# Fixed buffers for the transposed K chunks, and a writer that waits for the readers alone

## The chip, the core and the metric

The kernel runs on one core of a Trainium2 chip. The metric is the device time of one execution in microseconds (us).

## The reference

One decoding step: attention over a long cache, and an MLP beside it, mixed by a gate.

```python
B, Sq, D = 2, 1, 1024;  H, Sk, Dh = 32, 16384, 128      # all bf16
q = (x @ wq) per head
scores = einsum("bhqd,bhkd->bhqk", q, k_cache) * Dh**-0.5
a = (softmax(scores) @ v_cache) @ wo
b = mixer MLP of x with w1, w2, w3, w4
out = g * a + (1 - g) * b
```

The K and V caches hold 537 MB (2 x 2 x 32 x 16384 x 128 elements of 2 bytes). Every byte is used once, so the kernel has little arithmetic for each byte.

## The kernel before

The work is cut into 32 tiles, each of one batch and two heads. A tile loads 8.39 MB of K and 8.39 MB of V into a ring of three big buffers. K comes with its positions on the partitions, so VectorE transposes it in 32 x 32 blocks, in 16 chunks (`m`) of 128 x 1024 words, and TensorE multiplies each transposed chunk T with q in four matmuls. T has two buffers from a pool, so transpose `m` has to wait until the matmuls have read chunk `m - 2`.

```python
    tpool = ctx.enter_context(tc.tile_pool(name="tpool", bufs=2))

    def t_tile(shape, dtype, name="T"):
        return tpool.tile(shape, dtype, tag="T", name=name)
    # ... cut ...
        for m in range(NM):                               # NM = 16, per tile
            T = t_tile([P, 2, CJ, 32], FP32)
            nc.vector.transpose(
                out=T[:].rearrange("p w j s -> p j w s"),
                in_=Kw[:, m * CW : (m + 1) * CW].rearrange("p (j w e) -> p j w e", w=2, e=32),
            )
            # ... Tb is T seen as bf16 ...
            for v in range(4):
                nc.tensor.matmul(S[:], lhsT=z[:, v, NM - 1 - m : NM - 1 - m + P],
                                 rhs=Tb[:, v // 2, :, v % 2], ...)
```

After the 16 chunks come the softmax on 128 x 512 scores and, when V is there, 64 matmuls with V. Each load is issued when its buffer is free: the next V after the last transpose of a K, the next K after the matmuls of a V.

## Time and profile before

| | before |
|---|---|
| time, median | 1337.5 us |
| span in the profile | 1335.6 us |
| bytes moved | 573.3 MB, 429 GB/s |
| VectorE busy | 57%, of which the transposes of K 612 us |
| TensorE busy | 60% |

First the page of the kernel before. The rows of 40 digits cut the span into equal slices; a 9 stands for 90% or more. Below them are the DMA queues with their packets, megabytes, and share of the time of 16 DMA engines.

```profile
DMA  9999999999999999999999999999999999999997
GB/s 409 438 436 432 423 440 426 437 440 426 434 434 435 439 426 429 436 434 438 438 425 432 429 438 436 438 430 432 428 440 432 433 430 433 438 438 429 430 423 303
DMA packets 12725, 573.29 MB, mean 429 GB/s; under 512 B 1784, under 2 KB 1792, under 8 KB 2560
## 3 DMA queue, kind: packets, MB, share of 16 engines
q1 hardware_dynamic: 12664, 572.54, 99.2%
q8 instruction: 39, 0.64, 0.2%
q14 instruction: 14, 0.11, 0.0%
```

The DMA engines are full from the first slice to the last but one. Queue q1 carries the kernel's loads and alone fills 99.2% of the 16 engines.

The Trainium skill, "DMA: Bandwidth & Descriptors", section "Where 436 GB/s comes from", gives 435.2 GB/s as what the 16 ports between a core's DMA engines and its on-chip memory can carry. The trace agrees: most slices lie between 423 and 440 GB/s, and from one K to the next it is 435 GB/s (16.78 MB in 38.6 us).

Next the timeline of one tile: start, duration, engine and line, work, and in brackets how long the engine had idled and for what.

```profile
615.63 0.33 SPq L107 DMA_DIRECT2D Vn<-in_A_v_cache_dram  x1
...
620.38 0.33 SPq L96 DMA_DIRECT2D Kn<-in_A_k_cache_dram  x1
...
634.09 2.37 DVE L325 STREAM_TRANSPOSE T<-Kn 128x1024 f32<-128x1024 f32 x2 [7.35 <-DMA Kn<-in_A_k_cache_dram]
...
638.85 15.64 DVE L325 STREAM_TRANSPOSE T<-Kn 128x1024 f32<-128x1024 f32 x13 [0.22 <-PE S L333]
...
672.68 2.37 DVE L325 STREAM_TRANSPOSE T<-Kn 128x1024 f32<-128x1024 f32 x2 [7.06 <-DMA Kn<-in_A_k_cache_dram]
```

V is issued at 615.63 us, K at 620.38 us. VectorE idles 7.35 us until K lands at 634.09, and the next K lands 38.6 us later. The load issued at 615.63 stands behind one that is in flight until 634.09, so it could have been issued 18 us later without the engines running dry. The 13 transposes in 15.64 us (1.203 us each) run back to back.

Last, the line of the transposes: its instructions, those of the queue's sequencer (DVEq), and what VectorE idled for in front of it.

```profile
L325 DVE STREAM_TRANSPOSE T<-Kn x512: 1201/1245/1247, 43.5 to 1276.4; 128x1024 f32<-128x1024 f32 x171
L325 DVEq EVENT_SEMAPHORE  x449: 21/21/21, 44.8 to 1275.2; - x150
...
  DMA Kn<-in_A_k_cache_dram: 208.5, 30
```

### The profile page before, as it was taken

To read this page: it belongs to the slowest core of one execution; us is meant where nothing else is said; L and a number is where in the kernel's file an instruction comes from. 1 tells how busy PE (TensorE), PEld (TensorE's weight loads), DVE (VectorE), ACT (ScalarE), POOL (GpSimd) and SP (SyncE) were. 2 spreads that over 40 slices of the span, in tenths; PEclk is the share of its full clock that TensorE was granted. 3 is DMA by queue.
4 is the path that set the end of the run, shared out by engine and by line. 5 is a ranking of instruction groups with operands and counts; after the bars stand their busy time and mean duration, and the time that the engine had idled before them with its cause. 6 is when DMAs were issued, how large, how long until landed. Compare 5 with 4: busy or idle time off the path is not lost.

```text
span 1335.6 us, 11856 instructions
## 1 busy us (share of the span) xinstructions
PE 796.7 (60%) x4954; PEld 353.6 (26%) x5017; DVE 759.0 (57%) x998; ACT 27.2 (2%) x68; POOL 13.3 (1%) x40
## 2 busy tenths in 40 slices
PE   2576655676656665555666555576655556665564
PEld 0223222332225222222222222232222222222232
DVE  1677665466652665555666555566655556665540
ACT  0000000000000000000000000000000000000000
POOL 0000000000000000000000000000000000000000
PEclk9788877788776877778887777888777788877775
DMA  9999999999999999999999999999999999999997
GB/s 409 438 436 432 423 440 426 437 440 426 434 434 435 439 426 429 436 434 438 438 425 432 429 438 436 438 430 432 428 440 432 433 430 433 438 438 429 430 423 303
DMA packets 12725, 573.29 MB, mean 429 GB/s; under 512 B 1784, under 2 KB 1792, under 8 KB 2560
## 3 DMA queue, kind: packets, MB, share of 16 engines
q1 hardware_dynamic: 12664, 572.54, 99.2%
q8 instruction: 39, 0.64, 0.2%
q14 instruction: 14, 0.11, 0.0%
q10 hardware_dynamic: 8, 0.00, 0.0%
HBM read 572.53 MB, written 0.00 MB: 429 GB/s over the span
## 4 chain that ended last, share of the span: by engine, by line
DVE 25%; PE 25%; DMA 23%; issue 13%; another core or an unknown queue 12%; ACT 1%; SPq 0%; ACTq 0%; POOL 0%
DVE T L325 19%; PE S L333 14%; DMA Kn<-in_A_k_cache_dram 13%; PE O L377 7%; DMA wt<-in_B_w_dram 4%; DMA Vn<-in_A_v_cache_dram 3%; DMA wo<-in_A_wo_dram 3%; PE misc L212 2%; DVE Os L392 2%; PE misc L514 1%; ACT Pr L361 1%; DVE PT L365 1%; DVE mx L354 1%; PE misc L400 1%
## 5 line engine op out<-in xcount | busy, mean ns | idle before, releaser
L333 PE MATMUL S<-T,z 128*128 128x512 bf16 x1985 | 582.6, 422 | 333.4 <-DVE T L325 313.7
L325 DVE STREAM_TRANSPOSE T<-Kn 128x1024 f32<-128x1024 f32 x512 | 612.3, 1229 | 260.9 <-DMA Kn<-in_A_k_cache_dram 208.5
L333 PEld LDWEIGHTS <-z 128*128 128x128 bf16 x2048 | 211.0, 104 | 691.7 <-issue 530.0
L377 PE MATMUL O<-Vn,PT 128*32 128x512 bf16 x2048 | 121.4, 390 | 3.1 <-DMA Vn<-in_A_v_cache_dram 3.1
L377 PEld LDWEIGHTS <-PT 128*32 128x32 bf16 x2048 | 75.2, 142 | 48.2 <-issue 20.3
L388 DVE TENSOR_SCALAR Os<-O,xmask 128x128 f32<-128x128 f32 x32 | 11.2, 351 | 101.2 <-PE O L377 101.2
L212 PE MATMUL misc<-rs,ones_f 128*128 128x2 f32 x64 | 17.9, 349 | 79.1 <-DVE rs L408 79.1
L361 ACT ACTIVATE Pr<-S,nb 128x512 bf16<-128x512 f32 x32 | 22.0, 687 | 1199.1 <-DVE nb L356 1161.4
L344 DVE TENSOR_REDUCE m<-S 128x1 f32<-128x512 f32 x32 | 22.1, 692 | 36.9 <-PE S L333 36.9
L400 PE MATMUL misc<-asel,Os 128*128 128x2 f32 x64 | 12.4, 264 | 51.0 <-DVE Os L392 51.0
L365 DVE STREAM_TRANSPOSE PT<-Pr 128x512 bf16<-128x512 bf16 x32 | 22.8, 711 | 28.7 <-ACT Pr L361 28.7
L212 PEld LDWEIGHTS misc<-rs,ones_f 128*128 128x128 f32 x64 | 16.1, 312 | 84.0 <-issue 81.2
L392 DVE SCALAR_TENSOR_TENSOR Os<-O,xmask,Os 128x128 f32<-128x128 f32 x96 | 33.7, 351 | 3.4
L400 PEld LDWEIGHTS misc<-asel,Os 128*128 128x128 f32 x64 | 9.7, 191 | 65.2 <-DVE Os L392 61.0
L212 PE MATMUL misc<-mdiag,ones_f 128*128 128x128 f32 x64 | 15.5, 325 | 17.1 <-DVE mdiag L347 17.1
L354 DVE TENSOR_REDUCE mx<-misc 64x1 f32<-64x64 f32 x64 | 14.2, 222 | 19.1 <-PE misc L212 18.7
L301 POOL TENSOR_TENSOR z<-qsel,own 128x32 bf16<-128x32 bf16 x32 | 10.8, 337 | 1206.9 <-PE S L333 1177.1
L514 PEld LDWEIGHTS <-wt 128*128 128x128 bf16 x288 | 18.2, 171 | 9.2 <-DMA wt<-in_B_w_dram 8.3
L514 PE MATMUL misc<-xn2T,wt 128*128 128x2 bf16 x224 | 14.4, 202 | 8.1 <-DMA wt<-in_B_w_dram 8.1
L412 DVE RECIPROCAL rinv<-misc 128x2 f32<-128x2 f32 x32 | 5.5, 171 | 22.4 <-PE misc L212 22.4
L269 PE MATMUL misc<-wt,xT 128*2 128x512 bf16 x64 | 5.8, 541 | 19.5 <-DVE xT L257 19.5
L618 DVE CAST rows<-out_acc 128x256 bf16<-128x256 f32 x1 | 0.4, 425 | 29.6 <-PE out_acc L426 29.6
(83 smaller groups left out, 109.1 us busy)
## 6 DMA issues: line engine op xcount, KB each, us to landing
Vn<-in_A_v_cache_dram SPq DMA_DIRECT2D x2, 4096.0 KB, 47.1
wt<-in_B_w_dram SPq DMA_DIRECT2D x1, 7168.0 KB
w<-in_B_w_dram SPq DMA_DIRECT2D x4, 1792.0 KB, 31.3
wo<-in_A_wo_dram SPq DMA_DIRECT2D x6, 1024.0 KB, 33.1
wt<-in_B_w_dram SPq DMA_DIRECT2D x2, 2048.0 KB, 37.3
wo<-in_A_wo_dram SPq DMA_DIRECT2D x2, 512.0 KB, 18.7
wo<-in_A_wo_dram SPq DMA_DIRECT2D x4, 256.0 KB, 12.7
Kn<-in_A_k_cache_dram SPq DMA_DIRECT2D x32, 52.2
```

Of the source, the lines that this page charges most:

```text
L212: nc.tensor.matmul(ps[:], lhsT=ones_f[:], rhs=src, start=True, stop=True)
L325: nc.vector.transpose(out=T[:].rearrange("p w j s -> p j w s"), in_=Kw[:, m * CW : (m + 1) * CW].rearrange("p (j w e) -> p j w e", w=2, e=32),
L333: nc.tensor.matmul(S[:], lhsT=z[:, v, NM - 1 - m : NM - 1 - m + P], rhs=Tb[:, v // 2, :, v % 2], start=(m == 0 and v == 0), stop=(m == NM ...
L344: nc.vector.reduce_max(out=m[:], in_=S[:], axis=AX.X)
L354: nc.vector.reduce_max(out=mx[pa, :], in_=mall[pa, pa], axis=AX.X)
L361: nc.scalar.activation(out=Pr[:], in_=S[:], func=ACTF.Exp, bias=nb[:], scale=scale, accum_out=rs[:])
L365: nc.vector.transpose(out=PT[:], in_=Pr[:])
L377: nc.tensor.matmul(O[32 * g : 32 * g + 32, :], lhsT=PT[:, m : CJ * 32 : 16], rhs=V[:, j0 : j0 + 4, :], start=(m == 0), stop=(m == NM - 1),)
L388: nc.vector.tensor_scalar(out=Os[:], in0=Ox, scalar1=xmask[:, 0:1], scalar2=None, op0=ALU.mult)
L392: nc.vector.scalar_tensor_tensor(out=Os[:], in0=Ox, scalar=xmask[:, x : x + 1], in1=Os[:], op0=ALU.mult, op1=ALU.add,)
L400: nc.tensor.matmul(oc[:], lhsT=Os[:], rhs=asel[:], start=True, stop=True)
L514: nc.tensor.matmul(ps[:, c, :], lhsT=w[:, r, :].rearrange("k (p c) -> k p c", c=C)[:, :, c], rhs=actT[:, r, :], start=(r == 0), stop=(r == ...
```

## The change

The intent: transpose `m` needs the buffer that chunk `m - 2` used. Before, it waited for two things, TensorE's matmuls that read the chunk and VectorE's own earlier write. The matmuls could not have read before the write was done, so the second wait is implied by the first. With two fixed buffers in place of a pool the kernel can say so for that pair of instructions. The sizes and the alternation are the same.

```diff
-    tpool = ctx.enter_context(tc.tile_pool(name="tpool", bufs=2))
...
+    TW = 2 * CJ * 32
+    t_bufs = [const.tile([P, TW], FP32, name=f"T{n}") for n in range(2)]
+    t_next = [0]
+
+    def t_tile(shape, dtype):
+        buf = t_bufs[t_next[0] % 2]
+        t_next[0] += 1
+        # ... cut: a view of buf in the wanted type and shape
...
         for m in range(NM):
+            n = t_next[0] % 2
             T = t_tile([P, 2, CJ, 32], FP32)
-            nc.vector.transpose(
+            moved = nc.vector.transpose(
...
+            if m >= 2:
+                tc.declare_no_dep(
+                    moved.ins, t_writer[n], reason="implied by the wait for the readers"
+                )
+            t_writer[n] = moved.ins
```

The small users of T (gate masks, q rows, GELU, output rows) take the same two buffers.

More of the change, by code (lines that the diff above doesn't have):

```diff
@@ L75, in big_tile @@
         return big.tile([P, SLOT], BF16, tag="big", name=name)
-    def t_tile(shape, dtype, name="T"):
-        return tpool.tile(shape, dtype, tag="T", name=name)
+    TW = 2 * CJ * 32
[4 more added lines that the diff above has]
+        t_next[0] += 1
+        flat = buf[0 : shape[0], :]
+        if dtype != FP32:
+            flat = flat.bitcast(dtype)
+        flat = flat[:, 0 : int(np.prod(shape[1:]))]
+        dims = "abcd"[: len(shape) - 1]
+        sizes = dict(zip(dims[1:], shape[2:]))
+        return flat.rearrange(f"p ({' '.join(dims)}) -> p {' '.join(dims)}", **sizes)
     tiles = [(b, hg) for hg in range(NHG) for b in range(B)]
@@ L175 @@
     nc.vector.tensor_scalar(out=kill[:], in0=kill[:], scalar1=-1.0e30, scalar2=None, op0=ALU.mult)
-    osel = t_tile([P, 4, G], FP32, "osel")
+    osel = t_tile([P, 4, G], FP32)
     osel_f = osel[:].rearrange("p x a -> p (x a)")
@@ L260, in compute_q @@
         HB = CW // Dh
-        qrow = t_tile([P, 2, HB * 4, 2, 32], BF16, "qrow")
+        qrow = t_tile([P, 2, HB * 4, 2, 32], BF16)
         for t in range(2):
@@ L312 @@
     out_acc = acc.tile([P, QW], FP32, name="out_acc")
+    t_writer = {}
     S_tiles = {}
@@ L490, in gelu @@
         shape = list(pre_f32.shape)
-        sq = t_tile(shape, FP32, "gelu")
+        sq = t_tile(shape, FP32)
         nc.vector.tensor_tensor(out=sq[:], in0=pre_f32, in1=pre_f32, op=ALU.mult)
@@ L546, in st_mix @@
                 )
-        h1 = t_tile([P, HW], FP32, "h1")
+        h1 = t_tile([P, HW], FP32)
         nc.vector.tensor_copy(out=h1[0:64, :], in_=ps[0:64, :])
@@ L559, in st_up @@
     def st_up():
-        h2 = t_tile([P, FC, B], FP32, "h2")
+        h2 = t_tile([P, FC, B], FP32)
         nc.vector.tensor_copy(out=h2[:], in_=linear("w3", xn2T)[:])
@@ L615 @@
     assert not xfers
-    rows = t_tile([P, QW], BF16, "rows")
+    rows = t_tile([P, QW], BF16)
     nc.vector.tensor_copy(out=rows[:], in_=out_acc[:])
```

## The prediction

> **What bounds the kernel now: the load stream.** The page's slices show the DMA engines at 90% or more in 39 of 40 slices, at 409 to 440 GB/s in all but the last; span 1335.6 us, 573.29 MB, 429 GB/s on average. The Trainium skill, "DMA: Bandwidth & Descriptors", section "Where 436 GB/s comes from", gives a ceiling of 435.2 GB/s for a core's 16 engines; this trace sits on it. VectorE is busy 57%. In the timeline from 600 to 680 us, K lands at 634.09 and again at 672.68: 38.6 us for 16.78 MB, 435 GB/s. In each period VectorE idles 6 to 8 us until K lands (208.5 us in all in the groups list). The V load is issued at 615.63, right after the last transpose, while the K before it is in flight until 634.09; the next K at 620.38, with two loads still queued. So the queue is never empty: issues could come about 18 us (V) or 33 us (K) later before the engines ran dry.
>
> **What the change does.** T has the same two buffers and sizes. Transpose m drops its wait for transpose m-2, which the same engine did long before and which the wait for its readers implies. The trace shows 449 semaphore instructions of 21 ns on VectorE's queue at the transpose line: 14 per tile times 32, and one. A transpose waits for two things: the skill, "Perfetto Trace Analysis", section "Identifying Dependency Chains", says that instructions waiting on several engines may have an EventSemaphore put in front; the count fits. About 448 should vanish (9.4 us of queue time in all). Nothing is added.
>
> **What it is worth.** At full clock the transposes run back to back: 13 in 15.64 us, 1.203 us each, durations 1.201 to 1.247 us. If the extra instruction delays a start, the cadence can fall to perhaps 1.17 us (an estimate: neighbours overlap by about 0.04 us in half the cases, in the other half there is a gap); at most 0.5 to 0.8 us of a stage of 20 us. The first few transposes, at half clock, wait for TensorE (up to 0.9 us); that stays. All of the gain falls into the 6 to 8 us in which VectorE waits for K. Loads are issued that much earlier into a queue that holds work. The first transpose waits for K at 43.5 us; the tail is last V, w4, wo and the output rows, none of which the change touches. So nothing of it is on the critical path.
>
> **Predicted time: 1337.3 us**, range 1334 to 1340.5. Chances: faster by over 2% 0.01, within 2% 0.98, slower by over 2% 0.01.
>
> **Signs.** Right: semaphore instructions at the transpose line fall from 449 to near zero; transposes stay busy about 612 us; cadence 1.15 to 1.203 us; VectorE's idle time put down to the K load rises from 208.5 to 210 to 240 us; slices at 420 to 440 GB/s; K to K 38.6 us. Wrong: lower DMA share; the K wait vanishing; a longer cadence, from a new wait.
>
> **What would make it wrong.** If earlier issues changed how loads share the engines, the rate could move by tenths of a per cent either way. If the fixed buffers serialised the small users of T (gate, GELU), the tail could shift by a microsecond. For over 2% the load stream would have to be not the bound, which the wait for K in every period speaks against.

## More of the kernel before

Executions of one kernel agree within about 0.05% here. The 95% intervals given with the ratios below are wider, about 0.13% or 1.7 us to either side; where the text reads a smaller difference, it rests on ranges of four to six runs that don't touch, or it is called weak. The changed kernel was not timed again beside the experiments. The kernel before was, with medians of 1337.47, 1337.40 and 1337.56 us in three sets of rounds, so some 0.16 us of a comparison across sets can be drift.

Beside 512 transposes there are 449 semaphore instructions of 21 ns. By the trace's records 448 of them begin and end while a transpose is running.

## The result, and the profile after

| | before | after |
|---|---|---|
| time, median (6 runs each) | 1337.47 us | 1335.40 us |
| range of the runs | 1337.26 to 1337.66 | 1335.16 to 1335.62 |
| ratio | 1 | 0.9985, 95% interval 0.9972 to 0.9998 |
| instructions in the profile | 11856 | 11500 |
| semaphore instructions at the transposes | 449 | 1 |
| instructions recorded on VectorE's queue | 1454 | 1035 |

Ratios are the mean time of one kernel's runs over that of the other's of the same rounds, so not quite the ratio of the medians quoted. The verdict is "same" by the measure of 2%, and the time lies in the predicted range. But the ranges of the runs don't touch: 2.07 us are gone, of which the prediction had foreseen 0.2. The rest of this document is about those two microseconds.

(TensorE's matmul count on the page rises from 4954 to 5017. Some matmul records were missing in the first trace; the two programs have the same instructions for TensorE.)

The line of the transposes after:

```profile
L339 DVE STREAM_TRANSPOSE T<-Kn x512: 1201/1245/1247, 43.5 to 1274.0; 128x1024 f32<-128x1024 f32 x171
L339 DVEq EVENT_SEMAPHORE  x1: 21/21/21, 438.8 to 438.8; - x1
...
  DMA Kn<-in_A_k_cache_dram: 205.6, 30
```

The semaphore instructions went as intended. But 29 new ones came up at another line of VectorE, the first that reads the product with V (before, then after):

```profile
L388 DVEq EVENT_SEMAPHORE  x1: 21/21/21, 1288.6 to 1288.6; - x1
...
L408 DVEq EVENT_SEMAPHORE  x30: 21/21/21, 92.1 to 1286.2; - x30
```

So VectorE's queue has 448 - 29 = 419 instructions fewer. The transposes have the same durations, minimum, median and maximum. VectorE's wait for K did not grow by what it saved; it fell from 208.5 to 205.6 us.

The timeline after, the same tile:

```profile
615.83 0.33 SPq L119 DMA_DIRECT2D Vn<-in_A_v_cache_dram  x1
...
620.58 0.33 SPq L108 DMA_DIRECT2D Kn<-in_A_k_cache_dram  x1
...
633.27 2.37 DVE L339 STREAM_TRANSPOSE T<-Kn 128x1024 f32<-128x1024 f32 x2 [6.34 <-DMA Kn<-in_A_k_cache_dram]
...
639.77 14.38 DVE L339 STREAM_TRANSPOSE T<-Kn 128x1024 f32<-128x1024 f32 x12 [0.25 <-PE S L353]
...
671.85 2.37 DVE L339 STREAM_TRANSPOSE T<-Kn 128x1024 f32<-128x1024 f32 x2 [6.57 <-DMA Kn<-in_A_k_cache_dram]
```

Twelve transposes in 14.38 us are 1.20 us each, the cadence of before. The V load is issued at 615.83, no earlier than before (615.63), and K lands 0.8 us earlier than before. So the time was won by the load stream, and not because VectorE served it faster.

The page after, the same lines:

```profile
DMA  9999999999999999999999999999999999999997
GB/s 409 439 437 423 433 437 431 435 431 435 434 432 437 424 434 439 439 433 423 437 432 438 439 425 439 423 441 433 429 435 435 441 421 435 433 438 437 422 425 330
DMA packets 12722, 573.27 MB, mean 430 GB/s; under 512 B 1784, under 2 KB 1792, under 8 KB 2560
## 3 DMA queue, kind: packets, MB, share of 16 engines
q1 hardware_dynamic: 12664, 572.54, 99.4%
q8 instruction: 39, 0.64, 0.2%
q14 instruction: 11, 0.09, 0.0%
```

Nothing moved in the rows of digits. In the queues, q14 went from 14 packets to 11. The same loads fill 99.4% instead of 99.2% of a span that is 2.2 us shorter.

A caution about the chain of waits. Its line of shares by engine, before and then after:

```profile
DVE 25%; PE 25%; DMA 23%; issue 13%; another core or an unknown queue 12%; ACT 1%; SPq 0%; ACTq 0%; POOL 0%
```

```profile
PE 32%; DVE 29%; DMA 23%; another core or an unknown queue 12%; issue 2%; ACT 1%; SPq 0%; ACTq 0%; POOL 0%
```

"Issue" fell from 13% to 2%, 11% of the span or some 145 us, and the time fell by 2 us. The steps of the chain are put down to other causes when the semaphore instructions are gone. A chain says what was followed, not what would be won.

### Where the 2 us came from

In the second half of the kernel before, most K loads land 38.60 us after the one before, but every third one takes about 39.58 us. Three first transposes of neighbouring tiles of the kernel before, each started by the landing of K:

```profile
711.28 2.37 DVE L325 STREAM_TRANSPOSE T<-Kn 128x1024 f32<-128x1024 f32 x2 [6.39 <-DMA Kn<-in_A_k_cache_dram]
...
750.86 2.37 DVE L325 STREAM_TRANSPOSE T<-Kn 128x1024 f32<-128x1024 f32 x2 [7.79 <-DMA Kn<-in_A_k_cache_dram]
...
789.46 2.37 DVE L325 STREAM_TRANSPOSE T<-Kn 128x1024 f32<-128x1024 f32 x2 [6.39 <-DMA Kn<-in_A_k_cache_dram]
```

From 711.28 to 750.86 are 39.58 us, from 750.86 to 789.46 are 38.60. The same three after the change:

```profile
710.54 2.37 DVE L339 STREAM_TRANSPOSE T<-Kn 128x1024 f32<-128x1024 f32 x2 [6.92 <-DMA Kn<-in_A_k_cache_dram]
...
749.14 2.37 DVE L339 STREAM_TRANSPOSE T<-Kn 128x1024 f32<-128x1024 f32 x2 [6.24 <-DMA Kn<-in_A_k_cache_dram]
...
787.75 2.37 DVE L339 STREAM_TRANSPOSE T<-Kn 128x1024 f32<-128x1024 f32 x2 [6.52 <-DMA Kn<-in_A_k_cache_dram]
```

The two steps are 38.60 and 38.61 us. Not every step is so short after the change: of the twenty from 439 to 1216 us three take about 39.9 us (from 516.00, 826.50 and 1098.43), where before seven of twenty took 39.4 to 39.6. All twenty together take 776.8 us instead of 778.7. The slow steps of before fall together with a regular series among the packets of q14, one about every 117 us: at 502, 618, 735, 852, 969, 1085 and 1202 us, each followed by a K that lands about 1 us late. From the trace's DMA records, the packets around one of them, and around a packet of q8 (start in us, duration in ns, queue, bytes):

```
618.273    309  q14   8192      the program is fetched ...
618.579   2966  q1   65536      ... and the load packet behind it takes 2966 ns
618.280   2418  q1   65536      a load packet on another engine: 2418 ns
621.754    962  q8   16384
622.703   2886  q1   65536
```

A record doesn't name its DMA engine. But on an engine each packet starts some 4 ns ahead of the recorded end of the one before, so the records can be strung into 16 chains. (Where two engines happen to be at the same phase the stringing can swap them.) In the middle of the run no chain has a gap: every engine always works. The time between the ends of 16 load packets of one chain, one K and one V, is 38.64 us in nearly all places. It is 39.49 us where one packet of q14 lies between, and 40.06 us with one of q8. So **a fetch of 8 KB takes 0.85 us from one DMA engine, one of 16 KB 1.42 us.** A K can be used when the last of the 16 engines has done its part: for seven K loads looked up in e1 and in the changed kernel, the first transpose starts 0.4 to 0.5 us after the last chain's end. Since the queue is never empty, the engines don't wait for each other between loads: the one with the most fetches falls behind for good. As a mark serves the end of the last packets of 65536 bytes, which belong to the V of the last tile but one. (The last V comes in halves, in packets of 32768 bytes, and ends 19.4 us later on every chain that could be followed.) The sixteen chains reach this mark at (us from the span's start):

```
                          first engine   last engine   what the chains hold
before                        1265.9        1275.4     (identities swapped in places)
fixed buffers only (e1)       1266.0        1275.4     last: 11 fetches of q14, none of q8
after                         1265.9        1273.2     last: 4 or 5 fetches of q8
```

Seven engines carry next to none, eight share the fetches of q8 in turn, 4 to 5 each (5 x 1.42 = 7.1 us), and one carries those of VectorE, 11 x 0.85 = 9.4 us (three of the 14 packets of q14 lie on other engines). The 419 instructions fewer are three fetches fewer (11 to 8 on the chain that serves VectorE). That takes VectorE's engine from 9.4 to some 6.8 us, and now the eight engines with q8 are the last, at about 7.2 us. The difference, 9.4 - 7.2 = 2.2 us, is the gain. That is theory A.

That q8 serves TensorE, and q14 VectorE and GpSimd among others, is not written in the trace; the experiments show it by adding and removing instructions.

### The profile page after: what moved, and what is told of

Same layout as the page of the kernel before. It is cut to its first block, busy times and chain, and to the rows that moved or that the text cites. A ratio compares the mean times of both kernels' runs of the same rounds, so it can differ in the third digit from the quotient of the medians.

```text
span 1333.4 us, 11500 instructions
## 1 busy us (share of the span) xinstructions
PE 811.7 (61%) x5017; PEld 353.2 (26%) x5017; DVE 758.8 (57%) x998; ACT 27.2 (2%) x68; POOL 13.2 (1%) x40
## 3 DMA queue, kind: packets, MB, share of 16 engines
q1 hardware_dynamic: 12664, 572.54, 99.4%
## 4 chain that ended last, share of the span: by engine, by line
PE 32%; DVE 29%; DMA 23%; another core or an unknown queue 12%; issue 2%; ACT 1%; SPq 0%; ACTq 0%; POOL 0%
DVE T L339 22%; PE S L353 21%; DMA Kn<-in_A_k_cache_dram 13%; PE O L397 7%; DMA wt<-in_B_w_dram 4%; DMA Vn<-in_A_v_cache_dram 3%; DMA wo<-in_A_wo_dram 3%; PE misc L224 2%; DVE Os L412 2%; PE misc L534 1%; ACT Pr L381 1%; DVE PT L385 1%; DVE mx L374 1%; PE misc L420 1%
## 5 line engine op out<-in xcount | busy, mean ns | idle before, releaser
L353 PE MATMUL S<-T,z 128*128 128x512 bf16 x2048 | 597.4, 425 | 316.4 <-DVE T L339 301.7
L339 DVE STREAM_TRANSPOSE T<-Kn 128x1024 f32<-128x1024 f32 x512 | 612.2, 1229 | 258.8 <-DMA Kn<-in_A_k_cache_dram 205.6
```

Of the source, the lines that this page charges most:

```text
L339: moved = nc.vector.transpose(out=T[:].rearrange("p w j s -> p j w s"), in_=Kw[:, m * CW : (m + 1) * CW].rearrange("p (j w e) -> p j w e", ...
```

## The experiments

Theory A: the gain is the fetch traffic of the instructions that VectorE no longer has (448 at the transposes, 419 net), and it counts only on the DMA engine that ends last. Rival B: the dropped wait lets transposes, and so loads, start earlier. Rival C: the place of the fixed buffers, or how the small users share them. Each run below was timed in five rounds (four to six runs) against the kernel before, whose median was 1337.40 us in the rounds of e1 to e8 and 1337.56 in those of e9 to e11.

### e1: fixed buffers alone

```diff
-            if m >= 2:
-                tc.declare_no_dep(moved.ins, t_writer[n], reason=...)
```

> The two fixed buffers without the declaration: the build keeps both waits, and the 448 extra semaphore instructions on VectorE's queue. Theory A (the gain is three fewer fetches of VectorE's instructions over the DMA engine that ends last; each fetch of 8 KB takes about 0.86 us from it): as the kernel before, 1337.5 us, 10 such fetches in the middle of the run, ratio 1.000. Rival B (the dropped wait lets transposes, and so loads, start earlier): also as before. Rival C (where the fixed buffers lie, or how the small users of T share them, makes the gain): as the changed kernel, 1335.4 us, ratio 0.9985.

Measured: 1337.43 us, ratio 1.000 (0.9988 to 1.0013), 449 semaphore instructions, 14 packets on q14. The fixed buffers alone do nothing, so C falls. The chain that ends last holds 11 packets of q14, and no other engine holds more than one of these.

### e2: the instructions put back, without the wait

Where VectorE waits for K anyway, 14 copies of one column per tile:

```diff
+        for _ in range(14):
+            nc.vector.tensor_copy(out=scratch[:], in_=nb[:])
         PT_tiles[i] = PT
```

> The changed kernel with 14 copies of one column per tile on VectorE, put after each softmax where VectorE only waits for K. VectorE's queue has 1455 instructions again, as before (1456), but no transpose waits for its own engine. A: the gain is gone, 1337.4 us, 10 fetches by VectorE again. B and C: the gain stays, 1335.4 us.

Measured: 1337.42 us, ratio 1.0001 (0.9987 to 1.0015). Its queues:

```profile
q8 instruction: 39, 0.64, 0.2%
q14 instruction: 14, 0.11, 0.0%
```

The trace records 1453 instructions on VectorE's queue, against 1454 in the kernel before: with the copies the 30 semaphore instructions at the product with V went away again. The gain is gone, although no transpose waits for its own engine. The wait was worth nothing; the place that its instructions took in the program was worth the 2 us. B falls here.

### e3: twice as many

```diff
+        for _ in range(28):
+            nc.vector.tensor_copy(out=scratch[:], in_=nb[:])
```

> The same with 28 copies per tile, 1903 instructions on VectorE's queue. A: 13 fetches, six more than in the changed kernel, so the engine that serves them ends later than all others: 1340 us (1339 to 1341.5), 4.5 us above the changed kernel. B and C: 1335.4 us, or 1336 at most, because the copies fall into VectorE's wait for K.

Measured: 1341.23 us, ratio 1.0029 (1.0016 to 1.0041), 5.8 us above the changed kernel: at the upper end of what A gave. Queues, and the timeline around the last copies of a tile:

```profile
q8 instruction: 39, 0.64, 0.2%
q14 instruction: 18, 0.15, 0.0%
```

```profile
628.77 3.72 DVE L388 COPY scratch<-nb 128x1 f32<-128x1 f32 x20
635.17 2.37 DVE L340 STREAM_TRANSPOSE T<-Kn 128x1024 f32<-128x1024 f32 x2 [2.69 <-DMA Kn<-in_A_k_cache_dram]
```

Seven packets more than the changed kernel's 11 (the text said six). VectorE has done its copies and still waits 2.69 us for K, so the copies' own time doesn't hold up the loads. The last engine reaches the mark at 1279.3 us, the first at 1265.9, as in the other runs up to here.

### e4: the same copies on GpSimd

```diff
-            nc.vector.tensor_copy(out=scratch[:], in_=nb[:])
+            nc.gpsimd.tensor_copy(out=scratch[:], in_=nb[:])
```

> The same 28 copies per tile, on GpSimd instead of VectorE. A, with the part that only the DMA engine which ends last counts: GpSimd's fetches (6 in the middle of the run) go over another DMA engine; if that one carries few other fetches, it stays 2 us under the last, and the time is that of the changed kernel, 1335.4 us; if it is one of the eight that carry TensorE's fetches, the time is about 1340 us. A in a cruder form (every fetch costs the whole stream its time, whatever the engine): 1335.4 + 6 * 0.86, or a sixteenth of it, 1335.7 us. B and C: 1335.4 us.

Measured: 1335.34 us, ratio 0.9985 (0.9973 to 0.9998). The same copies that cost 5.8 us on VectorE's queue cost nothing on GpSimd's. Queues:

```profile
q8 instruction: 39, 0.64, 0.2%
q14 instruction: 19, 0.15, 0.0%
```

There are eight packets more here than in the changed kernel, one more than in e3. What counts is which engine serves them, not how many there are in all.

### e5: half of the transposes taken away (wrong)

```diff
-            T = t_tile(...); moved = nc.vector.transpose(...)
+            if m % 2 == 0:
+                T = t_tile(...); moved = nc.vector.transpose(...)
```

> Wrong result on purpose: the changed kernel with only every second transpose (the chunk of m is used for m and m + 1), so half of VectorE's largest item, some 306 us, is gone, and 256 more of its instructions. A: VectorE has 5 or 6 fetches instead of 7, but in the changed kernel the DMA engines with TensorE's fetches already end last (1273.2 us at the last V load, against 1272.7 for VectorE's), so nothing is gained: 1335.4 us, within 0.3. B (faster transposes pay): a clear gain of several us. The load stream as the bound: no gain.

Measured: 1335.34 us, ratio 0.9984 (0.9971 to 0.9998), against 0.9985 of the changed kernel: no gain. The group of the transposes (busy time, mean ns of one, idle time in front and its cause):

```profile
L340 DVE STREAM_TRANSPOSE T<-Kn 128x1024 f32<-128x1024 f32 x256 | 315.0, 1240 | 470.6 <-DMA Kn<-in_A_k_cache_dram 282.1
```

Of 612.2 us of VectorE's work 297.2 us are gone, and the wait for K grew from 205.6 to 282.1 us. None of these 297 us was on the critical path. Fetches for VectorE are fewer too (9 packets on q14), but its engine is no longer the last. The comparison with the reference is too coarse to see these errors in the attention part.

### e6: half of the PV matmuls taken away (wrong)

```diff
-        for m in range(NM):
+        for m in range(0, NM, 2):
```

> Wrong result on purpose: the changed kernel with half of the PV matmuls, so TensorE's queue has 2048 instructions fewer, 8 fetches of 16 KB fewer, one less on each of eight DMA engines (about 1.4 us each). A: VectorE's DMA engine is then the last: about 0.5 us gained, 1334.9 us (1334.5 to 1335.2). B and C: 1335.4 us.

Measured: 1334.99 us, ratio 0.9982 (0.997 to 0.9995). 0.4 us under the changed kernel, where A gave 0.5; but the runs of the two overlap (1334.68 to 1335.39, and 1335.16 to 1335.62), so by itself this is weak. The queues:

```profile
q8 instruction: 31, 0.51, 0.1%
q14 instruction: 11, 0.09, 0.0%
```

2048 instructions of TensorE fewer are 8 packets of q8 fewer: 256 instructions to a packet of 16 KB.

### e7: both cuts at once (wrong)

> Wrong result on purpose: both of these cuts at once. A: both kinds of DMA engine end earlier, about 1.5 us gained against the changed kernel, 1333.9 us (1333.4 to 1334.4), more than the sum of the two cuts alone. B and C: 1335.4 us, or as the half of the transposes alone.

Measured: 1333.91 us (1333.80 to 1334.02), ratio 0.9974 (0.996 to 0.9987). That is 1.5 us under the changed kernel, where the two cuts alone gave 0.1 and 0.4. Each cut alone lets one kind of engine end earlier and leaves the other as the last; only both move the end. Two costs that run side by side add up like a maximum, and this run shows it.

### e8: more instructions for TensorE

```diff
+        px = misc_psum([1, 1])
+        for _ in range(64):
+            nc.tensor.matmul(px[:], lhsT=zero[:], rhs=PT[:, 0:1], start=True, stop=True)
```

> The changed kernel with 64 weight loads and matmuls of one column per tile more on TensorE, after the softmax, where TensorE waits for K: 4096 instructions more, 16 fetches of 16 KB more, two on each of eight DMA engines. A: 2 * 1.42 = 2.8 us more, 1338.2 us (1337.5 to 1339), that is 0.7 ns for an instruction, a tenth of what one on VectorE's queue costs. B and C: 1335.4 us, the extra work being off the critical path.

Measured: 1338.13 us (1338.00 to 1338.23), 2.7 us above the changed kernel; A gave 2.8. The queues:

```profile
q8 instruction: 55, 0.90, 0.2%
q14 instruction: 11, 0.09, 0.0%
```

16 packets more on q8, spread over eight engines. An added instruction costs 0.7 ns here (2.7 us / 4096), against 6.7 ns in e3 (5.83 us over the 866 instructions by which VectorE's queue there exceeds the changed kernel's, 1901 against 1035 in the traces).

### e9: the cut of e6 in the kernel before (wrong)

> Wrong result on purpose: the kernel before, with half of the PV matmuls (8 fetches of TensorE's instructions fewer). A: in the kernel before the DMA engine with VectorE's 10 to 11 fetches ends last, and it carries none of TensorE's, so nothing is gained: 1337.4 us, within 0.3, although the same cut gained some 0.4 us in the changed kernel. A rival in which TensorE's work or its fetches cost the stream their time on average: the same gain as in the changed kernel or more.

Measured: 1337.40 us, ratio 1.000 (0.9987 to 1.0012), beside 1337.56 us of the kernel before in these rounds, with overlapping runs. No gain that stands out, as A has it: in the kernel before, the last engine holds none of TensorE's fetches. The same edit gains in one kernel and not in the other because another engine ends last.

### e10: the threshold on GpSimd

```diff
-        for _ in range(28):
+        for _ in range(56):
             nc.gpsimd.tensor_copy(out=scratch[:], in_=nb[:])
```

> 56 copies per tile on GpSimd instead of 28, so about 15 fetches over its DMA engine instead of 8. 28 per tile cost nothing (1335.3 us), because that engine then ended 3.5 us ahead of the last. A: it now passes the others, by 0.6 to 0.86 us for each fetch: 1336.5 to 1341 us, a threshold. If the copies on GpSimd simply don't matter to the load stream: 1335.4 us.

Measured: 1336.55 us (1336.45 to 1336.81), ratio 0.9993 (0.998 to 1.0007). That is 1.2 us above e4 (1.05 if the drift between the two sets of rounds is taken off), with runs that don't touch, and at the low end of what A allowed. The chain that ends last holds 14 packets of q14 and none of q8. The first 28 copies per tile were free and the second 28 were not. These 14 packets put their engine only 8.0 us behind the first, 0.57 us each, less than the 0.85 us of VectorE's. A fifteenth comes behind the mark, at 1295.4 us. The records show where the difference lies: the fetch itself takes 309 ns in both, but the load packet behind one of GpSimd's takes about 2.67 us instead of 2.96; why is open.

### e11: less to load

In the MLP's first half every shift moves the only row out at `Sq = 1`, so its result is zero whatever w1 and w2 hold (finite values taken for granted). This kernel leaves that half and its loads out:

```diff
-        layernorm(xT[:], xn1T[:])
-        w1 = wt.pop("w1")
-        # ... cut: its product, GELU and shifts
-        nc.vector.tensor_tensor(out=x1[:], in0=xT[:], in1=linear("w2", shT)[:], op=ALU.add)
+        nc.vector.tensor_copy(out=x1[:], in_=xT[:])
...
-        NT // 8: (lambda: load_rows(["w1", "w2"], [B_w1, B_w2]), st_mix),
+        NT // 8: (None, st_mix),                          # and no transfer where this is None
```

> A correct kernel: the changed one without the first half of the MLP, whose result is zero at one position (every shift moves the only row out), so w1 and w2 (4.19 MB) are not loaded. Load stream as the bound: 256 packets of 16 KB at 0.61 us over 16 DMA engines are 9.7 us, so 1325.7 us (1325 to 1326.5), ratio 0.991. If the engines' work or latency bounded the kernel: less, 1330 us or above.

Measured: 1325.81 us (1325.74 to 1325.97), ratio 0.9913 (0.9899 to 0.9926), 9.6 us under the changed kernel, and a correct kernel that beats both. Its queues:

```profile
q1 hardware_dynamic: 12376, 568.34, 99.3%
q8 instruction: 38, 0.62, 0.2%
q14 instruction: 11, 0.09, 0.0%
```

4.2 MB and 288 packets fewer on q1 (256 of data, the others signals of 4 bytes), and the time falls by what those bytes take on the engines. The gain has nothing to do with the change; it confirms that the stream of bytes is the bound, and it is what the change's own gain should be measured against.

### All runs in one table

The last column is from the profiled run of each; the mark is the end of the last packet of 65536 bytes, as above.

| run | time, us | packets q8 / q14 | last engine at the mark, us |
|---|---|---|---|
| before | 1337.47 | 39 / 14 | 1275.4 |
| after | 1335.40 | 39 / 11 | 1273.2 |
| e1 fixed buffers only | 1337.43 | 39 / 14 | 1275.4 |
| e2 VectorE +14 per tile | 1337.42 | 39 / 14 | 1275.2 |
| e3 VectorE +28 | 1341.23 | 39 / 18 | 1279.3 |
| e4 GpSimd +28 | 1335.34 | 39 / 19 | 1273.4 |
| e5 half the transposes | 1335.34 | 39 / 9 | 1273.6 |
| e6 half of PV | 1334.99 | 31 / 11 | 1272.7 |
| e7 both | 1333.91 | 31 / 9 | 1272.0 |
| e8 TensorE +128 per tile | 1338.13 | 55 / 11 | 1276.0 |
| e9 half of PV, before | 1337.40 | 31 / 14 | 1275.5 |
| e10 GpSimd +56 | 1336.55 | 39 / 25 | 1273.9 |
| e11 no w1, w2 | 1325.81 | 38 / 11 | 1263.5 |

The time minus the last column is 61.7 to 62.7 us in every row (the last V, the weights behind it, the output, and what lies outside the span). The number of packets alone does not order the times: e4 has five more than the kernel before and is 2.1 us faster.

## Why the prediction was right, and which step of it failed

- "What bounds the kernel now: the load stream." Right. In e5 half of VectorE's largest item is gone and nothing is gained; in e11 the time falls with the bytes.
- "About 448 should vanish." Right at the transposes: 449 became 1.
- "The cadence can fall to perhaps 1.17 us." Wrong: it is 1.20 us as before. The semaphore instructions were handled while a transpose ran (448 of 449 in the trace), so they cost VectorE nothing. The skill, "VectorE: DVE Perf Modes", section "The DRAIN you can't avoid", reports that eight copies took the same time with a semaphore after each as with one at the end; the cadence here agrees with it, and the prediction could have taken the hint.
- "VectorE's idle time put down to the K load rises from 208.5 to 210 to 240 us." Wrong: 205.6 us. Nothing was saved in the stage, and K came earlier.
- "Nothing is added", and "so nothing of it is on the critical path." The first is not quite so: 29 semaphore instructions came up at another line. The second is the step that failed. The argument counted what the removed instructions do on VectorE (9.4 us of queue time, all hidden) and left out what it takes to bring them to VectorE. The missing term of the sum is three fetches of 8 KB at 0.85 us on the engine that ended last, 2.6 us, of which 2.1 to 2.2 us count before other engines are the last. It was to be read in the profile of before: the lines of q8 and q14, and the K that lands 1 us late every third tile.
- The forecast of 1337.3 us with 1334 to 1340.5 held 1335.4 us. It held because the range was made wide for "the rate could move by tenths of a per cent", not because the cause was known.

What is open. Which physical DMA engine serves which queue was inferred from the chains, not read. A late K lands 0.98 us late where the fetch takes 0.85 us; the tenth between was not traced. Why the load packet behind one of GpSimd's fetches is held up less (so that the fetch costs 0.57 us) was not found, nor why the 29 semaphore instructions came up at the product with V. The declaration on the pool's buffers, without the fixed ones, was not tried.

## What to carry to other kernels

When every DMA engine is full from end to end, as here, the program itself is part of the load: its instructions are fetched by the same engines, and the time follows the one engine with the most to do. Then an instruction that costs its own engine nothing can still cost time, and one taken out pays only until another engine is the last. Before trusting "off the critical path", read the lines for instruction fetches among the queues, and ask whether a periodic delay in the landings has their period; the large gain, though, was in bytes that need not be loaded.

## What the Trainium skill lacked or had wrong

- "Runtime: NRT & Kernel Launch", section "Instruction fetch mechanics", says that crossing a block of 16 KiB (256 instructions) costs one DMA tail-bump, "mostly hidden". The block agrees for TensorE: 2048 instructions fewer are 8 packets of 16384 bytes fewer. VectorE's and GpSimd's fetches here are packets of 8192 bytes. And they are not hidden where the DMA engines are the bound: 1.42 us of one engine for 16 KB, 0.85 us for 8 KB, 2.0 us of the time for 418 instructions on VectorE (e2 against the changed kernel), 5.8 us for 866 (e3).
- "DMA: Bandwidth & Descriptors", section "Queues, rings and completion order", has queue row 14 for refills among the runtime's uses. In the kernel before, 39 of the instruction fetches (TensorE's) are on q8 and 14 on q14, if the profile's queue numbers are these rows, which no run shows.
- No page read tells how fetches are spread over the 16 DMA engines. Here TensorE's go over eight engines in turn, 4 to 5 each, and VectorE's all over one (11 of 11 in e1), so that the engines reach the same point up to 9.5 us apart (13.4 us in e3).
- No page read tells that a load packet behind a fetch takes longer itself: 2966 ns instead of 2418 behind 8 KB of VectorE's, about 2670 behind 8 KB of GpSimd's, 2886 behind 16 KB (single packets; others differ by up to some 100 ns).
